# The first batch of an FFT and channel-mix kernel: folds, stages and fillers put in another order

## The chip, the cores and the metric

The kernel runs on one core of a Trainium2 chip. The metric is the device time of one launch in microseconds (us); the median of several runs counts. Instructions of one engine run in the order in which they stand in its queue: PE (TensorE) multiplies, DVE (VectorE) and ACT (ScalarE) compute elementwise and empty PSUM, POOL (GpSimd) computes indices and issues the loads, SP (SyncE) issues the stores.

## The reference

```python
def _attn_ref(x) -> np.ndarray:          # x: 8 x 3072 x 256, float32
    X = np.fft.fft(x, axis=1)
    X = np.fft.fft(X, axis=2)
    return X.real.astype(np.float32)

def _moe_ref(x, mu_k, mu_r, w_k, w_v, w_r) -> np.ndarray:
    B, S, D = x.shape
    x_prev = np.concatenate([np.zeros((B, 1, D), dtype=np.float32), x[:, :-1, :]], axis=1)
    xk = mu_k * x + (1.0 - mu_k) * x_prev
    xr = mu_r * x + (1.0 - mu_r) * x_prev
    k = np.maximum(xk @ w_k, 0.0)
    v = k * k @ w_v
    r = 1.0 / (1.0 + np.exp(-(xr @ w_r)))
    return (r * v).astype(np.float32)
```

The second function takes the first one's result as x. So there is a real part of a two-dimensional Fourier transform of each of the 8 batches, then a mix of each row with the row before it, and three matrix products.

## The kernel before

**Fourier transform, for one batch.** Each batch is loaded in two halves h (0 and 1) as 96 partitions of some rows each: xp by plain loads, xm by gathers of the mirrored rows (lines 119 to 142, all on POOL). `fold` (L144, instructions at L153 and L155, DVE) adds xp and the mirrored xm into p. Stage A of the first batch is `a_sum` (L461, matmuls at L473): products of p with the table w_pm into PSUM, four rows at a time, emptied into the tile a by DVE (L434) or ACT (L436). Stage D (`d_units` L481, matmuls at L488) multiplies a by the table w_eo, two units (`d_half`) or four (`d_item`) at a time, into g_all. Stage C (`c_item` L513, matmuls at L526) multiplies g_all by the table m_cs for some of the 27 slots and empties PSUM into pq (ACT). With `turn_late` a one-row product stands in for a correction that `turned` (L507) makes in g_all later, by means of the table `turn` (L379 to 381). `halves` (L534, instruction at L542), `diff` (L545, L550) and a mix make the inputs x of the matrix products from pq, on DVE. The mix of the first batch's first part is `mix_part` (L579): one SCALAR_TENSOR_TENSOR for each half a (L586). Elsewhere it is `scaled` (L553, TENSOR_SCALAR at L562) and `mixed` (L566, TENSOR_TENSOR at L575).

**Channel mix.** Six chunks of 512 rows for each batch. `k_piece` (L611) takes the products with w_k (L606) in four steps of a chunk and puts them through Relu on ACT (L616); `square` (L620, instruction at L623) squares on DVE; `v_tile` (L637, L644) multiplies by w_v; `r_item` (L625, L630) makes the gate; `v_out` (L648) multiplies both on DVE and stores.

**The tables** w_pm, w_eo and m_cs are computed in the kernel: rows of small integers on DVE (L275 to 297), their outer products on PE (L301) into PSUM, angles u_w, rl and ueo on DVE (L241, which is the line of a helper), sines on ACT (L335 to 341 and L393).

**Fillers.** `keep_busy(n, ps, cols)` (L182, matmuls at L185) issues n matmuls of zeros of 512 or 128 columns; nothing reads their result.

**Order.** `pin_order` (L90) keeps each engine's instructions in the order in which the code issues them. Ahead of the loop (L666 to 734) the first batch's first stages stand written out by hand. In the loop (L813) each step issues a `k_piece`, then what `at(step, ...)` has entered for it, a `v_tile` and the squares; entries of kind "x" (stages A, C, D, `turned`, `r_item`) come ahead of the `v_tile`, others behind it. PSUM has three slots W of 1024 columns and two slots V of 512, handed out in turn.

Of the kernel before, what the change touches and what calls it, by code (L numbers as in the profile page):

```python
# [20 lines left out]
def _v(ap, extra_offset, free_dims):  # L21
    new_ap = [list(ap.ap[0])] + [[s, c] for (s, c) in free_dims]
    return dataclasses.replace(ap, offset=ap.offset + extra_offset, ap=new_ap)
# [16 lines left out]
def kernel(  # L40
# [41 lines left out]
    def ps_v():  # L82
        return ps_slot("V", 2, 512)
# [23 lines left out]
    V = nc.vector  # L107
# [74 lines left out]
    def keep_busy(n, ps, cols=512):  # L182

        for _ in range(n):
            nc.tensor.matmul(out=ps[:, 0:cols], lhsT=zeros,  # L185
                             rhs=_v(zeros, 0, [(0, cols // P), (1, P)]), start=True, stop=True)

    fill = ps_w()
    keep_busy(8, fill)


    mu_row = const.tile([2, 256], FP32)
# [46 lines left out]
    def ts(out, in0, s1, op0, s2=None, op1=None):  # L239
        kw = {} if op1 is None else {"op1": op1}  # L240
        V.tensor_scalar(out=out, in0=in0, scalar1=s1, scalar2=s2, op0=op0, **kw)  # L241
# [78 lines left out]
    def m_outer(ps, j0, j1):  # L320
        n = j1 - j0
        outer(ps[:, 0:64 * n], (Q2, rv(JR, j0, (1, n), (0, 64))),
              (RR, rv(TR, 0, (0, n), (1, 64))), (HQ, rv(ONE, 0, (0, 64 * n))))

    ang_ps = [ps_v(), ps_v()]
    m_outer(ang_ps[0], 0, NJ1)
    outer(prep[:, P_E:P_E + 128], (JR, rv(JR, 0, (1, 2), (2, 64))))
    m_outer(ang_ps[1], NJ1, NJ)
# [26 lines left out]
    ts(ueo, ueo, TURN - 1, ALU.bitwise_and)  # L355
    m_angles(ang_ps[1], NJ1, NJ)

    keep_busy(12, fill)
    ps = ps_v()
    for a in range(2):  # L360
        nc.tensor.matmul(out=ps[:, 2 * a:2 * a + 2], lhsT=mu_p[:, a], rhs=unit, start=True,
                         stop=True)
    V.tensor_copy(out=mu_f.rearrange("p a i -> p (a i)"), in_=ps[:, 0:4])

# [9 lines left out]
               32.0 - 64.0 * c, ADD)  # L376
        ts(rv(TO, 15, (32, 4)), _v(one, 15, [(32, 4)]), 0.0, ADD)

    def turn_table(ps):  # L379
        V.tensor_copy(out=cols, in_=ps[:, 0:2])  # L380
        ts(turn, ramp, cols[:, 0:1], ALU.is_equal, cols[:, 1:2], MUL)

    def rows():
# [48 lines left out]
    def evac(out_ap, in_ap, eng):  # L432
        if eng == "V":
            V.tensor_copy(out=out_ap, in_=in_ap)  # L434
        else:
            nc.scalar.activation(out=out_ap, in_=in_ap, func=AF.Copy)  # L436
# [24 lines left out]
    def a_sum(b, h, i0, eng="A", m=4):  # L461


        if (h, i0) == (0, 0):
            a_tile(b)
        ps = ps_w() if m == 4 else ps_v()
        for i in range(m):
            parts = [(h, i0 + i + 1 - h, 0, 2 * WA, 0, 1)]
            if h and i0 + i == 7:
                parts = [(0, 0, 0, WA, WA, 1), (1, 7, 1, WA, 1, 2)]  # L470
            for half, q, o, n, w, step in parts:
                for k in range(2):
                    nc.tensor.matmul(out=_v(ps, 256 * i + o, [(2 * WA // n, n)]),  # L473
                                     lhsT=p_t[b, half][:, q, 128 * k:128 * k + 128],
                                     rhs=_v(w_pm[0:96], (WA + WB) * k + w,
                                            [(WA + WB, 2), (step, n // 2)]),
                                     start=(k == 0), stop=(k == 1))
        evac(_v(a_t[b], 8 * h + i0, [(16, 2 * WA), (1, m)]),
             _v(ps, 0, [(1, 2 * WA), (256, m)]), eng)

    def d_units(b, ps, u0, n, bank):  # L481

# [94 lines left out]
                        op=ALU.subtract if m else ALU.add)  # L577

    def mix_part(b, j, lo, hi):  # L579


        if lo == 0:
            x_t[b, j, 0] = mix_pool.tile([P, 2, 1536], FP16, name=f"x{j}0")
        n = 64 * (hi - lo)
        for a in range(2):
            V.scalar_tensor_tensor(out=x_t[b, j, 0][:, a, 64 * lo:64 * hi],  # L586
                                   in0=_v(x_t[b], 64 * (26 * a + lo), [(1, n)]),
                                   scalar=mu_f[:, a, j:j + 1],
                                   in1=_v(y_t[b], 64 * (NSL * a + lo), [(1, n)]),
                                   op0=ALU.mult, op1=ALU.add)  # L590
# [77 lines left out]
    eo_sine()  # L668
    eo_rest()
    m_sine(NJ1, NJ2)  # L670
    m_sine(NJ2, NJ)
    keep_busy(4, fill)
    fold(0, 0, 1, 4)
    a_sum(0, 0, 0, "V")
    fold(0, 0, 5, 4)
    a_sum(0, 0, 4)
    loads()
    fill = ps_v()
    keep_busy(10, fill, 128)
    fold(0, 1, 0, 4)  # L680
    a_sum(0, 1, 0)
    keep_busy(4, fill, 128)
    fold(0, 0, 0, 1)
    fold(0, 1, 4, 4)
    a_sum(0, 1, 4, "V", 2)
    a_sum(0, 1, 6, "A", 2)
    turn_rows()
    ps = ps_w()
    keep_busy(6, ps, 128)
    d_half(0, 0, ps_v(), "A")  # L690
    d_half(0, 2, ps_v(), "V")
    for n in range(2):
        outer(ps[:, n:n + 1], (TO + n, rv(ONE, 0, (1, 1))))
    keep_busy(6, ps[:, 512:1024], 128)
    turn_table(ps)
    c_item(0, 0, 5, "A", True)
    c_item(0, 5, 4, "A", True)
    d_item(0, 1)

# [25 lines left out]
    diff(0, 0, 4)  # L727
    mix_part(0, 0, 0, 4)
    halves(0, 5, 9)
    keep_busy(10, ps_w(), 128)  # L730
    k_products(chunks[0], 0, 0, 256)
    k_products(chunks[0], 1, 0, 256)
    diff(0, 4, 8)
    mix_part(0, 0, 4, 8)
    c_item(0, 9, 4, "A", True, True)
    c_item(0, 13, 4, "A", True, True)
    for n, c in enumerate(chunks):
        at(4 * n + (4, 5, 6)[(n < 3) + (n == 0)], r_item, c)

# [2 lines left out]
    at(0, diff, 0, 8, 16)  # L742
    at(0, mix_part, 0, 0, 8, 16)
    at(4, loads_2)
    at(4, d_item, 0, 2)
    at(4, d_item, 0, 3)
    at(4, mix_part, 0, 1, 0, 8)
    at(5, turned, 8, 13)
    at(5, c_item, 0, 17, 8)
    at(5, mirrored_mu)  # L750
    at(5, mix_part, 0, 1, 8, 16)
# [107 lines left out]
```

## Time and profile before

| | us |
|---|---|
| median of 3 runs | 445.52 (445.05 to 446.3) |
| the profiled execution, its own time | 449.81 |
| its span, first to last instruction | 448.0 |
| busy in the span: PE / PEld / DVE / ACT / POOL | 436.6 / 311.8 / 361.0 / 327.5 / 51.6 |

The profile is of one execution. The mean granted clock of PE is 0.988 of full speed over the span. A row of a timeline gives the start, the time from the first instruction's start to the last one's end, engine, line, operation, what it writes and reads, shape and count, and in brackets the engine's idle time before it and what ended it. A row of a group gives busy time, mean duration in ns and idle time before. "x8" counts instructions.

### The profile page before, as it was taken

To read this page: it belongs to the slowest core of one execution; us is meant where nothing else is said; L and a number is where in the kernel's file an instruction comes from. 1 tells how busy PE (TensorE), PEld (TensorE's weight loads), DVE (VectorE), ACT (ScalarE), POOL (GpSimd) and SP (SyncE) were. 2 spreads that over 40 slices of the span, in tenths; PEclk is the share of its full clock that TensorE was granted. 3 is DMA by queue.
4 is the path that set the end of the run, shared out by engine and by line. 5 is a ranking of instruction groups with operands and counts; after the bars stand their busy time and mean duration, and the time that the engine had idled before them with its cause. 6 is when DMAs were issued, how large, how long until landed. Compare 5 with 4: busy or idle time off the path is not lost.

```text
span 448.0 us, 8503 instructions
## 1 busy us (share of the span) xinstructions
PE 436.6 (97%) x3479; PEld 311.8 (70%) x3479; DVE 361.0 (81%) x521; ACT 327.5 (73%) x377; POOL 51.6 (12%) x66
## 2 busy tenths in 40 slices
PE   9798999999999999999999999999999999999995
PEld 3665677677777767777777777777777777676664
DVE  6559999989699887989789887989789755997453
ACT  7558988677777777777777877777777777666661
POOL 7842312001200040001200010000000000000000
PEclk9779999999999999999999999999999999999999
DMA  7994758236823295234932363323223233233334
GB/s 129 173 208 78 149 93 180 51 70 109 171 60 68 50 160 128 53 72 84 184 70 50 71 126 63 67 53 72 62 58 71 48 72 64 55 72 71 72 68 97
DMA packets 34507, 40.93 MB, mean 91 GB/s; under 512 B 3906, under 2 KB 30788, under 8 KB 34468
## 3 DMA queue, kind: packets, MB, share of 16 engines
q1 hardware_dynamic: 27524, 25.05, 24.9%
q0 software_dynamic: 6784, 15.21, 21.2%
q8 instruction: 27, 0.44, 0.4%
q10 hardware_dynamic: 160, 0.13, 0.1%
q14 instruction: 12, 0.10, 0.1%
HBM read 30.41 MB, written 25.17 MB: 124 GB/s over the span
## 4 chain that ended last, share of the span: by engine, by line
PE 91%; DVE 7%; ACT 1%; issue 1%
PE psV L644 35%; PE psW L606 34%; PE psW L630 9%; PE psW L526 3%; PE psW L488 2%; PE psW L185 2%; PE psW L456 2%; DVE k L623 1%; DVE x L586 1%; DVE p L153 1%; DVE d L550 1%; PE psW L473 1%; PE psV L301 1%; DVE o L654 0%; DVE y L542 0%
## 5 line engine op out<-in xcount | busy, mean ns | idle before, releaser
L616 ACT ACTIVATE rl<-psW 128x1024 f16<-128x1024 f32 x192 | 196.1, 1024 | 98.3 <-PE psW L606 93.8
L606 PE MATMUL psW<-x,wk 128*128 128x512 f16 (+1 forms) x776 | 197.7, 377 | 2.2 <-ACT rl L616 0.7
L644 PE MATMUL psV<-wv_sb,k 128*128 128x256 f16 x1536 | 199.3, 273 | 0.3 <-DVE k L623 0.2
L644 PEld LDWEIGHTS <-k 128*128 128x128 f16 x1536 | 146.0, 98 | 28.6 <-DVE k L623 1.1
L623 DVE TENSOR_TENSOR k<-rl 128x2048 f16<-128x2048 f16 (+1 forms) x98 | 117.4, 1200 | 50.5 <-ACT rl L616 46.5
L606 PEld LDWEIGHTS <-wk 128*128 128x128 f16 x776 | 75.7, 98 | 53.2 <-issue 3.2
L654 DVE SCALAR_TENSOR_TENSOR o<-psV,r 128x512 f32<-128x512 f32 (+1 forms) x97 | 66.1, 682 | 16.2 <-PE psV L644 13.7
L575 DVE TENSOR_TENSOR x<-y,t 128x1536 f16<-128x1536 f16 x60 | 57.5, 959 | 2.1
L630 PE MATMUL psW<-wr,x 128*128 128x256 f16 x384 | 49.8, 273 | 0.0
L635 ACT ACTIVATE r<-psW 128x1024 f16<-128x1024 f32 x48 | 48.9, 1018 | 0.8 <-PE psW L630 0.8
L630 PEld LDWEIGHTS <-x 128*128 128x128 f16 x384 | 37.6, 98 | 14.6 <-issue 0.3
L125 POOL DMA_INDIRECT xm<-in_x_dram,idx x25 | 31.5, 1260 | 8.1 <-issue 7.2
L122 POOL DMA_DIRECT2D xp<-in_x_dram x16 | 9.1, 567 | 199.0 <-DVE p L155 184.3
L436 ACT ACTIVATE g_all<-psW 128x1024 f16<-128x1024 f32 (+3 forms) x39 | 28.1, 724 | 1.2 <-PE psW L488 1.2
L436 ACT ACTIVATE pq<-psW 128x768 f16<-128x768 f32 (+5 forms) x32 | 27.5, 860 | 2.0 <-issue 1.3
L436 ACT ACTIVATE a<-psW 128x832 f16<-128x832 f32 x30 | 25.8, 860 | 3.1 <-PE psW L473 3.1
L542 DVE TENSOR_TENSOR y<-pq 128x960 f16<-128x960 f16 (+5 forms) x38 | 18.7, 533 | 3.9 <-ACT pq L436 3.7
L526 PEld LDWEIGHTS <-g_all 128*128 128x128 f16 (+1 forms) x216 | 15.3, 99 | 8.9 <-ACT g_all L436 1.1
L153 DVE TENSOR_TENSOR p<-xp,xm 96x2304 f16<-96x2304 f16 (+3 forms) x19 | 20.9, 1102 | 0.0
L562 DVE TENSOR_SCALAR t<-d,mu_m 128x1536 f16<-128x1536 f16 x32 | 19.8, 619 | 0.0
L488 PEld LDWEIGHTS <-a 128*128 128x128 f16 x208 | 14.7, 101 | 7.4 <-issue 0.7
L526 PE MATMUL psW<-m_cs,g_all 128*128 128x128 f16 (+2 forms) x204 | 18.1, 227 | 0.9 <-ACT g_all L436 0.9
(98 smaller groups left out, 195.7 us busy)
## 6 DMA issues: line engine op xcount, KB each, us to landing
out_dram<-o SPq DMA_DIRECT2D x190, 128.0 KB, 2.4
xp<-in_x_dram POOLq DMA_DIRECT2D x8, 432.0 KB
xp<-in_x_dram POOLq DMA_DIRECT2D x8, 384.0 KB
wv_sb<-in_moe_w_v_dram POOLq DMA_DIRECT2D x1, 512.0 KB
xm<-in_x_dram,idx POOLq DMA_INDIRECT x25
out_dram<-o ACTq DMA_DIRECT2D x2, 64.0 KB
out_dram<-o SPq DMA_DIRECT2D x2, 64.0 KB
wk<-in_moe_w_k_dram,row_i POOLq DMA_INDIRECT x4
```

The lines of the kernel that those rows point to most:

```text
L125: nc.gpsimd.indirect_dma_start(dst, None, src, bass.IndirectOffsetOnAxis(ap=idx, axis=0))
L153: V.tensor_tensor(out=p[:, q0:q0 + n], in0=xp[:, q0:q0 + n], in1=_v(xm, o + 256, [(-256, n), (-1, 256)]), op=ALU.add)
L436: nc.scalar.activation(out=out_ap, in_=in_ap, func=AF.Copy)
L526: nc.tensor.matmul(out=ps[0:m, o:o + 64 * k], lhsT=g_all[:, u, 128 * min(f, 1):128 * min(f, 1) + m], rhs=m_cs[:, f % 2, sl:sl + k], start= ...
L575: V.tensor_tensor(out=dst, in0=_v(y_t[b], 64 * (NSL * a + lo + 3 * m), [(1, n)]), in1=_v(x_t["t", a], 64 * lo, [(1, n)]), op=ALU.subtract ...
L606: nc.tensor.matmul(out=st["k", ds][:, 512 * hs + lo:512 * hs + hi], lhsT=wk_sb[m][a][:, 128 * fc:128 * fc + 128], rhs=xk[:, a, 512 * i + l ...
L616: nc.scalar.activation(out=st["rl"][:, 2 * ds:2 * ds + 2], in_=st["k", ds].rearrange("p (f t) -> p f t", f=2), func=AF.Relu, bias=0.0, sca ...
L623: V.tensor_tensor(out=k2_t[c][:, lo:hi], in0=r, in1=r, op=ALU.mult)
L630: nc.tensor.matmul(out=ps[:, 256 * tb:256 * tb + 256], lhsT=x_t[b, 1, m][:, a, 512 * i + 128 * tb: 512 * i + 128 * tb + 128], rhs=wr_sb[m] ...
L635: nc.scalar.activation(out=st["r", c], in_=ps, func=AF.Sigmoid)
L644: nc.tensor.matmul(out=st["v", tb - h][:, 256 * h:256 * h + 256], lhsT=k2_t[c][:, fc, 128 * tb:128 * tb + 128], rhs=wv_sb[:, fc], start=(f ...
L654: V.scalar_tensor_tensor(out=o.rearrange("p a b -> p (a b)")[:, 0:256 * n], in0=st["v", t0][:, 0:256 * n], scalar=16.0, in1=st["r", c][:, ...
```

## The change

The early part of the first batch is put in another order, and the counts of fillers differ:

- Fillers: ahead of the outer products 4 instead of 8 (512 columns), and one more between them; ahead of the product for mu 5 instead of 12, and 7 behind it; 16 + 6 + 6 of 128 columns along stage A instead of 4 (of 512 columns) and 10 + 4 + 6 + 6; 20 instead of 10 ahead of the first `k_products`.
- Stage A of half 0: matmuls and evacuation of the first four rows are apart (`a_evac`). On DVE the second fold stands ahead of the evacuation, on PE the second `a_sum` comes directly behind the first, and on ACT the last pair of sines (`m_sine(NJ2, NJ)`) behind that second one's evacuation.
- Stage D of units 0 to 7 at once in four `d_half`, the last two in one PSUM tile; before, units 4 to 7 came as a `d_item` behind the first stage C pieces.
- Stage C of slots 0 to 16 directly behind it; before, slots 9 to 16 came behind the first `k_products`.
- The table `turn`: its two products in step 1 and its DVE operation in step 2 of the loop. The other `d_item` one step earlier (3), `turned` too (4).
- `mix_part` outside the first eight rows of the first part (five calls) by `scaled` and `mixed`.

```diff
-    keep_busy(8, fill)
+    keep_busy(4, fill)
...
     ang_ps = [ps_v(), ps_v()]
+    keep_busy(1, fill)
...
-    keep_busy(12, fill)
+    keep_busy(5, fill)
...
+    keep_busy(7, fill)
...
-    def turn_table(ps):
+    def turn_cols():
+        ps = ps_w()
+        for n in range(2):
+            outer(ps[:, n:n + 1], (TO + n, rv(ONE, 0, (1, 1))))
         V.tensor_copy(out=cols, in_=ps[:, 0:2])
+
+    def turn_table():
         ts(turn, ramp, cols[:, 0:1], ALU.is_equal, cols[:, 1:2], MUL)
...
+        a_ps[b, h, i0] = ps
+        if eng:
+            a_evac(b, h, i0, eng, m)
+
+    a_ps = {}
+
+    def a_evac(b, h, i0, eng, m=4):
         evac(_v(a_t[b], 8 * h + i0, [(16, 2 * WA), (1, m)]),
-             _v(ps, 0, [(1, 2 * WA), (256, m)]), eng)
+             _v(a_ps[b, h, i0], 0, [(1, 2 * WA), (256, m)]), eng)
...
     def mix_part(b, j, lo, hi):
+        if j or lo > 4:
+            for a in range(2):
+                scaled(b, j, 0, a, lo, hi)
+                mixed(b, j, 0, a, lo, hi)
+            return
...
     m_sine(NJ1, NJ2)
+    fold(0, 0, 1, 4)
+    a_sum(0, 0, 0, "")
+    fold(0, 0, 5, 4)
+    a_evac(0, 0, 0, "V")
+    a_sum(0, 0, 4)
     m_sine(NJ2, NJ)
-    keep_busy(4, fill)
-    fold(0, 0, 1, 4)
-    a_sum(0, 0, 0, "V")
-    fold(0, 0, 5, 4)
-    a_sum(0, 0, 4)
     loads()
     fill = ps_v()
-    keep_busy(10, fill, 128)
+    keep_busy(16, fill, 128)
     fold(0, 1, 0, 4)
     a_sum(0, 1, 0)
-    keep_busy(4, fill, 128)
+    keep_busy(6, fill, 128)
...
     turn_rows()
-    ps = ps_w()
-    keep_busy(6, ps, 128)
+    keep_busy(6, ps_w(), 128)
     d_half(0, 0, ps_v(), "A")
     d_half(0, 2, ps_v(), "V")
-    for n in range(2):
-        outer(ps[:, n:n + 1], (TO + n, rv(ONE, 0, (1, 1))))
-    keep_busy(6, ps[:, 512:1024], 128)
-    turn_table(ps)
+    ps = ps_w()
+    for u, eng in ((4, "A"), (6, "V")):
+        d_half(0, u, ps[:, 256 * u - 1024:256 * u - 512], eng)
     c_item(0, 0, 5, "A", True)
     c_item(0, 5, 4, "A", True)
-    d_item(0, 1)
+    c_item(0, 9, 4, "A", True, True)
+    c_item(0, 13, 4, "A", True, True)
...
-    keep_busy(10, ps_w(), 128)
+    keep_busy(20, ps_w(), 128)
...
-    c_item(0, 9, 4, "A", True, True)
-    c_item(0, 13, 4, "A", True, True)
...
-    at(4, d_item, 0, 2)
-    at(4, d_item, 0, 3)
+    at(1, turn_cols)
+    at(2, turn_table)
+    at(3, d_item, 0, 2)
+    at(3, d_item, 0, 3)
     at(4, mix_part, 0, 1, 0, 8)
-    at(5, turned, 8, 13)
+    at(4, turned, 8, 13)
```

## The prediction

> **What bounds the kernel now.** I read the page first (the slices, then the chain that ended last by engine), then the chain in order of time, then clock and transfers in short windows, then the timelines of DVE, PE and ACT up to 55 us.
>
> ```profile
> PEclk9779999999999999999999999999999999999999
> PE 91%; DVE 7%; ACT 1%; issue 1%
> ```
> ```profile
> 49.56 1.14 DVE k L623
> ...
> 52.64 0.87 PE psV L644 x8
> ```
>
> 91% of the chain is PE; in order of time the chain leaves DVE at about 50.7 and from 52.64 on is almost all PE. Matmuls behind that point are untouched by the change, so what is won before it moves the end. The start is another matter: the clock is low in slices 1 and 2, and there the chain changes engine at nearly every step. The windows (columns: busy of PE, PEld, DVE, ACT, POOL, then clock, DMA share, GB/s) say where:
>
> ```profile
> 17.00:18.00 1.00, 1.00 (x10) 0.92 (x8) 0.77 (x2) 0.62 (x1) 0.76 (x1) 0.52 1.36 177
> 27.00:28.00 1.00, 0.96 (x12) 0.77 (x11) 1.00 (x4) 0.43 (x1) 0.70 (x2) 0.86 1.00 197
> ```
> ```profile
> 1.00 3.59 PE L185 MATMUL psW<-zeros 128*128 128x512 f16 x8 [1.00 <-DVE xm L208]
> 5.62 0.31 PE L301 MATMUL psW<-rw 1*128 1x128 f16 x1
> 7.14 4.27 PE L185 MATMUL psW<-zeros 128*128 128x512 f16 x12
> 11.87 1.04 PE L185 MATMUL psW<-zeros 128*128 128x512 f16 x4
> 15.83 0.89 PE L473 MATMUL psW<-w_pm,p 96*128 96x208 f16 x8 [1.93 <-DVE p L155]
> 17.17 1.59 PE L473 MATMUL psW<-w_pm,p 96*128 96x208 f16 x8
> 18.98 2.24 PE L473 MATMUL psV<-w_pm,p 96*128 96x208 f16 x10
> 22.12 1.04 PE L488 MATMUL psV<-w_eo,a 128*128 128x128 f16 x8 [0.25 <-issue]
> 29.08 1.12 PE L526 MATMUL psV<-m_cs,g_all 128*128 128x128 f16 x12
> ```
>
> A share of 0.52 in the window from 17 and 0.86 in that from 27 put the half clock at 17.04 to 27.28, 10.24 us. It follows the idle stretch of 1.93 us ahead of 15.83. The price is plain: the same eight matmuls take 0.89 us at 15.83 and 1.59 at 17.17. Fillers show a slow start too: 0.45 us each at 1.00 (3.59 / 8), 0.26 at 11.87, though the clock column has 1.00 there; full speed begins inside the twelve at 7.14. The Trainium skill, page "TensorE: Matmul & The Clock Gate", Part 1, says that the clock is judged over a free-running window of about 3.41 us, low by default, full after a busy window; 10.24 us are three such windows, so by that rule the trace agrees.
>
> DVE is the other line; brackets give idle time and what ended it:
>
> ```profile
> 3.14 0.37 DVE L241 TENSOR_SCALAR rw<-rw 1x64 f16<-1x64 f16 x1
> 5.96 0.37 DVE L241 TENSOR_SCALAR u_w<-psW 128x26 int32<-128x26 f32 x3 [2.46 <-PE psW L301]
> 10.93 0.69 DVE L241 TENSOR_SCALAR rl<-rl 128x1024 int32<-128x1024 int32 x1
> 12.06 0.69 DVE L153 TENSOR_TENSOR p<-xp,xm 96x1024 f16<-96x1024 f16 x1
> 13.94 1.02 DVE L434 CAST a<-psW 128x832 f16<-128x832 f32 x1 [0.98 <-PE psW L473]
> 15.69 0.68 DVE L153 TENSOR_TENSOR p<-xp,xm 96x1024 f16<-96x1024 f16 x1
> 17.63 0.17 DVE L155 TENSOR_TENSOR p<-xp,xm 96x4 f16<-96x4 f16 x1
> 25.71 0.63 DVE L542 TENSOR_TENSOR y<-pq 128x320 f16<-128x320 f16 x2 [1.08 <-ACT pq L436]
> 31.77 0.76 DVE L542 TENSOR_TENSOR y<-pq 128x512 f16<-128x512 f16 x2 [2.28 <-ACT pq L436]
> 34.63 2.48 DVE L623 TENSOR_TENSOR k<-rl 128x1024 f16<-128x1024 f16 x4
> 37.04 1.40 DVE L586 SCALAR_TENSOR_TENSOR x<-d,mu_f,y 128x512 f16<-128x512 f16 x2
> ```
>
> From 25.71 to 50.7 DVE idles once for long, 2.28 us ahead of 31.77, until the pq of the late stage C pieces. So there DVE sets the pace, and whatever moves 25.71 forward moves the rest.
>
> **The change part by part.**
>
> *Fillers ahead of the tables.* Eight become four, one is added behind the small products: three fewer ahead of the product at 5.62, on which u_w waits 2.46 us. At 0.43 to 0.45 us each that is 1.3: u_w starts at 4.66. Its inputs allow it: the last row of rw is done at 3.51, the product now starts at 4.3. DVE's work behind u_w has no other wait, so the last mask ends at 10.3, not 11.62; the mu products stand behind five fillers, not twelve, and are done by about 8.7, so the copy to mu_f no longer waits. First fold: 12.06 becomes 10.4.
>
> *Is the data there?* In the order of the queue the first two folds need 432 and 384 KB.
>
> ```profile
> xp<-in_x_dram POOLq DMA_DIRECT2D x8, 432.0 KB
> xp<-in_x_dram POOLq DMA_DIRECT2D x8, 384.0 KB
> ```
> ```profile
> 5.00:10.00 5.00, 5.00 (x14) 1.70 (x13) 3.90 (x14) 3.64 (x9) 3.65 (x12) 1.00 0.97 175
> 10.00:15.00 5.00, 3.79 (x22) 1.92 (x20) 3.59 (x8) 4.70 (x9) 4.39 (x5) 1.00 1.09 172
> ```
>
> At 175 GB/s 875 KB come between 5 and 10 alone, so these 816 are there at 10.4 even if nothing came before 5. The other half needs 768 more and a gather of single rows (some 48): at 172 GB/s all of it by 14.4 on the same bound, and earlier by what did come before 5; those folds are due at 13.2 to 14.5. POOL's and SP's order is unchanged. So I cost the loads at nothing; if they came after all, each microsecond late is a microsecond lost.
>
> *Folds ahead of the evacuation.* Now the second fold waits behind the CAST (13.94, itself waiting 0.98 for PE), and PE idles 1.93. After: folds at 10.4 and 11.2, PE's first product 11.35 to 12.25 and its second directly behind, the CAST at 12.3 to 13.3. The three folds left take 2.11 us (15.69 to 17.80), so the last ends at 15.3 instead of 17.80: 2.5 earlier. On ACT two sines move behind the second evacuation; they delay only the third, which is done before the last one.
>
> *The clock.* From 11.3 on PE has products and fillers with only sub-microsecond gaps, so I take full clock from about 10 to 12 us on. From the last fold to stage D took 4.32 us (17.80 to 22.12): PE came late from its slow products, and ten matmuls took 2.24. After: 1.12 for the ten, and ACT's 0.54:
>
> ```profile
> 21.52 0.54 ACT L436 ACTIVATE a<-psV 128x416 f16<-128x416 f32 x1 [1.86 <-PE psV L473]
> 24.98 1.44 ACT L436 ACTIVATE pq<-psW 128x640 f16<-128x640 f32 x2 [1.34 <-issue]
> 30.65 1.08 ACT L436 ACTIVATE pq<-psV 128x512 f16<-128x512 f32 x2 [2.06 <-PE psV L526]
> ```
>
> with hand-offs 1.9 us, so stage D starts at 17.2, 4.9 earlier.
>
> *Stage D of eight units, stage C of 17 slots.* Stage D to the first y took 3.59 us (22.12 to 25.71). After, the instruction order holds a new wait: the last half's matmuls write the PSUM tile that ACT is reading for the third half, and all of stage C stands behind them on PE. So: 0.4 for the first half, 1.1 for ACT's two evacuations of 512 columns (two in 1.08 at 30.65), 0.3 for the last half, 0.6 for six matmuls of C, 0.72 for pq, 0.1 of hand-offs: 3.2. First y at 20.4, 5.3 earlier. The four pq are done by 22; DVE asks for the last two at 24.1, so the 2.28 goes. Next late would be ACT's Relu for the squares, four times 1.0 from about 24.5, ready as DVE takes them up.
>
> *DVE up to the squares.* Its own work from first y to squares is 34.63 - 25.71 - 2.28 = 6.6; then 2.4 for the squares and 0.35 for the two table operations that move between them (DVE was idle where they stood). They end at 20.4 + 6.6 + 2.4 + 0.35 = 29.8 instead of 37.04: 7.2 earlier. Can PE keep up?
>
> ```profile
> 25.00:30.00 5.00, 4.58 (x44) 3.41 (x42) 3.64 (x10) 2.30 (x3) 3.97 (x5) 0.77 1.07 208
> 30.00:35.00 5.00, 3.70 (x21) 1.72 (x22) 3.16 (x6) 4.35 (x6) 0.00 (x0) 1.00 1.14 209
> 35.00:40.00 5.00, 3.84 (x35) 2.21 (x33) 4.96 (x10) 3.73 (x6) 0.00 (x0) 1.00 0.09 17
> ```
>
> From 25 to 40 it was busy 12.1 us, 1.1 of it the price of the half clock up to 27.28; ten fillers more are 0.9 (0.093 each by the twelve at 29.08): 11.9. DVE needs 14.3 - 2.28 + 0.5 = 12.5 for the same stretch. DVE stays the bound, narrowly.
>
> *Mixes in two operations.* Five parts, ten pairs:
>
> ```profile
> L586 DVE SCALAR_TENSOR_TENSOR x<-d,mu_f,y 128x512 f16<-128x512 f16 x10 | 7.0, 742 | 0.1
> ```
> ```profile
> L562 DVE TENSOR_SCALAR t<-d,mu_f 128x1536 f16<-128x1536 f16 x28 | 17.1, 611 | 0.0
> L550 DVE TENSOR_TENSOR d<-y 128x512 f16<-128x512 f16 x2 | 0.8, 424 | 0.1
> L539 DVE TENSOR_SCALAR pq<-pq 1x64 f16<-1x64 f16 x7 | 1.1, 162 | 0.0
> ```
>
> One operation costs 0.66 to 0.70 in the row (two in 1.40, overlapping). The pair is a TENSOR_SCALAR of 512, between 0.16 (64) and 0.61 (1536), by the line between them 0.30, then 0.04 of waiting for it and 0.34 for the addition: 0.68. Ends: 0.54 to 0.99, so -1.4 to +3.3 us over ten; I take +0.03 each, 0.3 in all. The Trainium skill, "VectorE: DVE Perf Modes", section on the TRN2 errata, speaks against splitting: a fixed cost per instruction, about 150 cycles of 0.96 GHz as measured there; by it the scaling would be some 0.29 us (an estimate from that page) and the sum the same.
>
> *Sum.* 7.2 - 0.3 = 6.9. I give back 0.9 for hand-offs that the records do not explain: at 30.65 ACT starts both pq, though PE's twelve matmuls end at 30.20 and the first six about 0.5 before. So 6.0: span 448.0 to 442.0, the profiled execution 449.81 to 443.8. The timed runs (445.05 to 446.3) lie 4.3 below that execution; I take the difference as the same in both kernels: 445.52 - 6.0 = **439.5 us**.
>
> **The rivals.**
>
> *The clock rises a step later.* Fewer fillers up front, and the mu products (0.6 us, two rows) cut the later row. If full clock comes at 17 instead of 10 to 12, four products lose 0.7 each, of which the CAST and the folds pass on 0.7, the product of the second half 0.7, and its late hand-offs 0.7 to 1.0: 2.2 less, 441.7. For it: the twelve fillers at 7.14 were unbroken. The skill's clock page asks for about 4 us without a break, and the unbroken stretches here are shorter; by that rule this rival holds. Against: the break is small, and the window ending at 27.28 released the clock with a mix of small matmuls. Chance 0.13.
>
> *The timed runs of before had less half clock than the profiled one.* Then only the order is won: 2 to 3 us (folds 1.6, the 2.28, less what the clock hid): 443. For it: timed runs lie 4.3 lower. Against: they agree within 1.25. Chance 0.08.
>
> *The pairs cost their upper end,* 3.3: 442.5, and more of the same if DVE work that was hidden behind 52 us comes to the front. 0.05.
>
> *Slower: full clock does not come before about 34 us.* PE's 3.6 us of products up to first y become 7.2, with late hand-offs as above, so y comes at 25.0, 0.7 earlier than before; with the 2.28 and less 0.6 for table operations and pairs DVE's line is 2.4 ahead. But PE's margin of 0.6 is soon gone, and then each microsecond at half clock costs half of one. The lead and the margin, 3.0, are used up at a release 6 us behind y, at 31; with one at 34 to 36 the time is 447 to 448. For it: behind 17 us the clock stayed low for two windows in which PE looked nearly full. Against: 48 fillers, where there were 36, stand behind the second product. 0.04.
>
> *The change does not do what it says:* excluded by the instruction order, in which both folds stand ahead of the CAST.
>
> **How the numbers follow.** Forecast (438 to 441.2) 0.68; the rivals 0.13, 0.08, 0.05, 0.04; 0.02 is left for more than 7.5 us. The range takes in the first three rivals in part: 437.6 to 443.3. Under 0.3% (1.3 us) a measurement of this kernel can't tell from no change: faster 0.91, same 0.05 (parts of the second and third), slower 0.04.
>
> **What would show it.** In the profile after: u_w near 4.7; first fold near 10.4; no idle of over 1 us on PE between 12 and 17; clock 1.00 from 13 on at the latest; stage D near 17.2; first y near 20.4, no idle over 1 us on DVE up to the squares; their end near 30; the pairs at 0.68. Wrong if 0.5 shows behind 17, if DVE waits for pq or data, or if the lead at 30 us is lost by 84.

## The result and the profile after

The changed kernel takes **444.23 us** (median of 6, 443.51 to 444.68) against 445.51 (445.05 to 446.3) for the kernel before in the same set: ratio 0.9969, 95% interval 0.9956 to 0.9982. The gain is 1.3 us, where 6.0 had been forecast.

The profiled executions tell another story: span 448.0 before and 441.7 after, 6.3 less, and the forecast had 6.0 less. The timed medians do not follow, and the experiments below show that the agreement of the spans is largely luck: the profile of the kernel before has late hand-offs (results of PE that reach their reader well behind the product's end), that of the changed kernel has none, and this is not the change's doing. The page of the changed kernel, granted clock by slices and shares of the chain:

```profile
PEclk9999999999999999999999999999999999999999
PE 86%; DVE 5%; DMA 4%; POOL 2%; issue 1%; ACT 1%; POOLq 0%
```

The two slices at 7 are gone, and the chain now leads through DMA and POOL for 6% of the span, which it did not before: in the start-up it now hangs on loads. The timelines of DVE and of PE, after (start, length, ..., idle before and what ended it):

```profile
4.88 0.37 DVE L241 TENSOR_SCALAR u_w<-psW 128x26 int32<-128x26 f32 x3 [1.38 <-PE psW L301]
10.42 0.68 DVE L153 TENSOR_TENSOR p<-xp,xm 96x1024 f16<-96x1024 f16 x1
13.10 1.02 DVE L441 CAST a<-psW 128x832 f16<-128x832 f32 x1 [1.00 <-PE psW L480]
15.95 0.17 DVE L155 TENSOR_TENSOR p<-xp,xm 96x4 f16<-96x4 f16 x1
16.75 0.59 DVE L441 CAST a<-psV 128x416 f16<-128x416 f32 x1 [0.62 <-PE psV L480]
21.11 0.56 DVE L556 TENSOR_TENSOR y<-pq 128x320 f16<-128x320 f16 x2 [0.48 <-ACT pq L443]
24.74 0.75 DVE L556 TENSOR_TENSOR y<-pq 128x512 f16<-128x512 f16 x2
26.26 0.35 DVE L576 TENSOR_SCALAR t<-d,mu_f 128x512 f16<-128x512 f16 x1
26.64 0.42 DVE L589 TENSOR_TENSOR x<-y,t 128x512 f16<-128x512 f16 x1
26.99 0.35 DVE L576 TENSOR_SCALAR t<-d,mu_f 128x512 f16<-128x512 f16 x1
29.24 1.29 DVE L642 TENSOR_TENSOR k<-rl 128x1024 f16<-128x1024 f16 x2
```
```profile
12.18 1.59 PE L480 MATMUL psW<-w_pm,p 96*128 96x208 f16 x16
16.18 1.07 PE L480 MATMUL psV<-w_pm,p 96*128 96x208 f16 x10
17.88 0.34 PE L502 MATMUL psV<-w_eo,a 128*128 128x128 f16 x3 [0.30 <-ACT a L443]
```

Read down the first column: the first fold at 10.42 (forecast 10.4), the last fold done at 16.12 (15.3), stage D at 17.88 (17.2), first y at 21.11 (20.4), the third y at 24.74 without a wait, squares done at 30.53 (29.8). From the CAST on all of it is 0.7 to 0.8 us later than forecast.

Behind the first stored tile both kernels are alike. The rows of the output's first issue, before and after:

```profile
47.79 2.40 SPq L662 DMA_DIRECT2D out_dram<-o  x3
```
```profile
41.56 1.36 SPq L681 DMA_DIRECT2D out_dram<-o  x2
```

From there to the end it is 448.0 - 47.79 = 400.2 and 441.7 - 41.56 = 400.1 us, and 400.1 to 400.2 in every other trace but that of c_ahead_held (400.9). **The time is the start-up plus a constant**, so an execution of 445.5 has its first issue near 43.6. And in every execution whose span is listed the time lies 1.7 to 1.9 us above it, so spans and times tell the same. The kernel before was profiled in an execution 4.3 us above its median, the changed one in its fastest of six.

### The profile page after: what moved, and what is told of

Its sections match the earlier page's. It is cut to its first block, busy times and chain, and to the rows that moved or that the text cites. A ratio compares the mean times of both kernels' runs of the same rounds, so it can differ in the third digit from the quotient of the medians.

```text
span 441.7 us, 8525 instructions
## 1 busy us (share of the span) xinstructions
PE 431.9 (98%) x3484; PEld 309.4 (70%) x3484; DVE 361.0 (82%) x532; ACT 326.7 (74%) x377; POOL 50.9 (12%) x66
## 4 chain that ended last, share of the span: by engine, by line
PE 86%; DVE 5%; DMA 4%; POOL 2%; issue 1%; ACT 1%; POOLq 0%
PE psV L663 36%; PE psW L625 35%; PE psW L649 9%; DMA xp<-in_x_dram 2%; PE psW L502 2%; PE psW L540 2%; PE psW L463 2%; DMA wr<-in_moe_w_r_dram,row_i 2%; DVE k L642 1%; POOL xm L125 1%; DVE x L589 1%; POOL wk L125 1%; DVE d L564 1%; DVE p L153 1%; DVE t L576 1%
## 5 line engine op out<-in xcount | busy, mean ns | idle before, releaser
L589 DVE TENSOR_TENSOR x<-y,t 128x1536 f16<-128x1536 f16 (+1 forms) x70 | 61.8, 882 | 2.4
L443 ACT ACTIVATE g_all<-psW 128x1024 f16<-128x1024 f32 (+4 forms) x39 | 27.7, 712 | 0.0
L576 DVE TENSOR_SCALAR t<-d,mu_f 128x1536 f16<-128x1536 f16 (+1 forms) x38 | 20.6, 542 | 0.1
```

The costliest lines, as they stand in the source:

```text
L576: V.tensor_scalar(out=dst, in0=src, scalar1=mu, scalar2=None, op0=ALU.mult)
L589: V.tensor_tensor(out=dst, in0=_v(y_t[b], 64 * (NSL * a + lo + 3 * m), [(1, n)]), in1=_v(x_t["t", a], 64 * lo, [(1, n)]), op=ALU.subtract ...
```

## The experiments

The question: what did that execution of the kernel before have that the others lack, and what is each part of the change worth without it? The five sets ran on four chips, on which the kernel before took 449.4 to 450.4 us: as much as the profiled 449.81, and not the 445.5 of the result. The record names no chip for the result and the first two profiles. Times are compared within a set, and where they are not, the text says so. The recorded ratios can differ from the quotient of the medians by up to 0.0024 (after_again: 448.75 / 450.28 is 0.9966), so differences of 1 us between sets mean little.

| kernel | us, median (range) | ratio to the kernel before (95%) |
|---|---|---|
| before_again | 449.72 (446.93 to 451.31) | 0.9968 (0.9935 to 1.0002) |
| after_again | 448.75 (448.29 to 450.99) | 0.9988 (0.9959 to 1.0017) |
| before_cover | 450.59 (448.74 to 456.35) | 1.0011 (0.9981 to 1.0041) |
| after_one_op | 448.61 (447.36 to 449.68) | 0.9969 (0.9941 to 0.9998) |
| after_look | 448.53 (448.14 to 449.39) | 0.9983 (0.9958 to 1.0008) |
| held_loads | 444.93 (444.3 to 445.53) | 0.9889 (0.9846 to 0.9932) |
| wide_fill | 446.49 (445.84 to 448.08) | 0.9943 (0.9915 to 0.9971) |
| stage_a | 448.86 (446.74 to 452.78) | 0.999 (0.9955 to 1.0025) |
| before_held | 446.4 (445.7 to 447.21) | 0.9931 (0.9911 to 0.9951) |
| stage_a_held | 443.91 (443.58 to 444.73) | 0.9878 (0.9856 to 0.9899) |
| one_op_held | 444.84 (444.3 to 446.77) | 0.9903 (0.9879 to 0.9926) |
| wide_held | 445.09 (444.25 to 445.83) | 0.9904 (0.9885 to 0.9923) |
| dc_held | 447.47 (446.42 to 448.29) | 0.9932 (0.9908 to 0.9956) |
| c_ahead_held | 445.19 (443.14 to 445.56) | 0.986 (0.9825 to 0.9894) |
| stage_a_held_2 | 444.1 (443.53 to 445.38) | 0.9856 (0.9821 to 0.9891) |
| held_loads_2 | 445.23 (444.75 to 445.57) | 0.9877 (0.9843 to 0.991) |
| eight_early | 443.88 (443.47 to 444.17) | 0.9885 (0.9849 to 0.992) |
| four_early | 443.21 (443.01 to 443.57) | 0.9868 (0.9833 to 0.9904) |

### Both kernels once more, more cover, one operation

before_again and after_again are the two kernels unchanged. The other two edits:

```diff
 (before_cover)
     fold(0, 0, 1, 4)
     a_sum(0, 0, 0, "V")
+    keep_busy(8, fill)
     fold(0, 0, 5, 4)
```
```diff
 (after_one_op)
-        if j or lo > 4:
-            for a in range(2):
-                scaled(b, j, 0, a, lo, hi)
-                mixed(b, j, 0, a, lo, hi)
-            return
```

> The kernel before, unchanged, run again. Theory A (the profiled execution of before was an unlucky one, with 10.24 us at half clock in the middle, and most executions have less): the runs' spans stand at 443.2 to 444.7 us, each about 1.8 below its time, with a mean clock above 0.99, and a new profile shows a shorter half-clock stretch or one in another place. Theory B (the profiler adds some 4 us to before and not to the kernel after, or the lead is lost in executions without a profile): the new profile shows 448 us again with a clock near 0.988, while the times stay at 445.5.

> The changed kernel, unchanged, run again. Theory A: spans of 441.5 to 443, clock 0.997 to 1.0; time of the median 444.2; the first r product of the loop near 36 us. Theory B: the same.

> The kernel before with eight fillers of 512 columns in PE's idle stretch of 1.93 us ahead of the second stage A product; nothing else. Theory A (half clock costs the start its time whenever that idle falls badly): no half clock behind 13 us in any execution, the first r product near 39 to 40 us instead of 42.46, times 1 to 2 us below the ordinary runs of before and with less scatter, about 444. Theory C (ordinary executions of before have full clock there anyhow): the time is that of before, 445.5, within 0.5.

> The changed kernel with mix_part in one operation everywhere, as before. By the pair's price of the prediction (+0.03 us each, eight of them ahead of 52 us): 0.2 to 0.3 us faster than the kernel after, so 443.9. Rival: the pairs cost up to 0.33 each in effect, or gain by freeing something else: then 2 us faster or slower.

The second trace of the kernel before has half clock from 14.5 to 17.9 only, not 10.2 us of it; its first fold stands at 10.94, not 12.06. With a third of the half clock its time is nearly the same (449.34 against 449.81), so the half clock alone doesn't make those 4.3 us. Neither theory's numbers came: here both kernels take longer, and by about as much, 449.7 against 445.5 and 448.75 against 444.2. And the changed kernel's second trace has something that its first has not: PE stops for 2.18 us inside the last products of stage A, and stage D starts at 21.65. Eight fillers more did nothing (half clock came all the same, from 22.2 to 29.0 us), and of the one-operation form nothing is told apart (0.14 us between the medians). The next set was made to find that stop.

### What stops TensorE: the loads or its own instructions

after_look is the changed kernel; stage_a is the kernel before with the front half of the change alone (fillers of the front, folds first, 16 and 6 fillers). The two others:

```diff
 (held_loads, on the changed kernel)
-        load_xh(1, 0)
         for a in range(2):
             gather(wr_sb[0][a], moe_w_r, row_i[:, a:a + 1])
-        load_xh(1, 1)
...
+    def late_loads():
+        x_tiles(1, 0)
+        V.memset(xp_t[1, 0][0:1, 0, 0:1], 0.0)
+        load_p(1, 0)
+        load_m0(1)
+        load_m(1, 0, 0, 8, idx_8[:, 1, 0:1])
+        load_xh(1, 1)
...
     mix_part(0, 0, 4, 8)
+    late_loads()
```
```diff
 (wide_fill, on the changed kernel)
-    keep_busy(16, fill, 128)
+    keep_busy(4, fill)
...
-    keep_busy(20, ps_w(), 128)
+    keep_busy(5, ps_w())
```

> The changed kernel unchanged, for its trace and the clocks of its executions beside those of the kernel before on one chip. Every trace so far has its end 400.15 to 400.23 us behind the first output's issue, so the time is the start-up alone. Theory U (the profiled execution of the kernel before was out of the ordinary: its half clock and its late hand-offs cost 4 us more than in its other executions, and the change gains the order only): 0.996 to 0.9985 of the kernel before, the first y at 21 to 22 us where TensorE's results are handed over promptly. Theory N (the forecast of 6.0 us holds wherever the kernel before is undisturbed too): 0.987. If hand-offs are late here as in the second look at this kernel (2.18 us idle in the last products of stage A), the first y comes at 25 to 26.5 us and the clock has a half stretch of 6.8 us.

> The changed kernel with the loads of x for the second batch held back behind the second mix of the first one (wk, wv and wr still load at once). Theory L (TensorE's results reach the other engines late, by 0.7 to 2.9 us between 16 and 30 us, because these loads run then): the idle 2.18 us in the last products of stage A is gone, the first y at 21 to 22 us, and 2 to 4 us less than the changed kernel on the same chip if that one shows late hand-offs there; the same within 0.5 us if it shows none. Rival F (TensorE's own stream of instructions is what arrives late, as it runs out of the 8 KB that it last fetched): the idle time stays, the same within 0.7 us. Fold of the second batch has 15 us between the loads' new start and its use, so no wait there.

> The changed kernel with its small fillers of 128 columns (16, 6, 6 and 20) as a quarter as many of 512 columns (with a 256 for the odd half): the same columns, 35 fewer products and as many fewer weight loads ahead of the first chunk. Rival F (the stream of instructions): the idle time ahead of the last products of stage A goes or moves behind stage D, and 1 to 3 us less than the changed kernel where that shows it. Theory L (the loads): the idle time stays at the same place and the time is the same within 0.7 us. Fillers in the wide form end no sooner, so a gain has no other source.

> The kernel before with the front half of the change alone: the fillers of the front placed anew, both folds ahead of the evacuation, 16 and 6 fillers; stages D and C, the half of c_item behind the second mix and the one-operation mixes stay as they were. Theory U (order only, small): the last fold ends 1.7 to 2.5 us sooner than in the kernel before, stage D begins as much sooner, but the second half of stage C is still behind the second mix, so the squares gain less than stage D: 0.995 to 1.000 of the kernel before. Theory N (the forecast's step: 2.5 us at the last fold, and the clock a step sooner, carried whole): 0.990 to 0.994.

On one chip, held_loads takes 3.6 us less than the changed kernel, wide_fill 2.0 less. The timelines of the changed kernel (after_look), PE and then DVE:

```profile
17.03 0.52 PE L480 MATMUL psV<-w_pm,p 96*128 96x208 f16 x4
18.88 0.70 PE L480 MATMUL psV<-w_pm,p 96*128 96x208 f16 x6 [1.32 <-PE psV L480]
20.96 0.62 PE L502 MATMUL psV<-w_eo,a 128*128 128x128 f16 x8 [1.06 <-DVE rw L374]
```
```profile
19.59 0.59 DVE L441 CAST a<-psV 128x416 f16<-128x416 f32 x1 [2.74 <-PE psV L480]
25.40 0.56 DVE L556 TENSOR_TENSOR y<-pq 128x320 f16<-128x320 f16 x2 [0.48 <-issue]
```

The four products end at 17.55; DVE, idle since 16.85, may take them only at 19.59. **The result is handed over 2.0 us late**, where the profile of the changed kernel at the top has 0.04 (products done at 16.71, CAST at 16.75). The lateness is in PE's signal: the trace's semaphore records have it at 19.57. PE itself waits in the same way, by the program's waits for its own filler that used that PSUM slot: that is the 1.32. What ACT and DVE hand over is prompt in the same trace: stage D starts 0.06 us behind ACT's evacuation, 20.36 to 20.90. The same place in held_loads:

```profile
16.91 1.06 PE L486 MATMUL psV<-w_pm,p 96*128 96x208 f16 x10
```
```profile
17.48 0.65 DVE L447 CAST a<-psV 128x416 f16<-128x416 f32 x1 [0.62 <-PE psV L486]
21.86 0.56 DVE L562 TENSOR_TENSOR y<-pq 128x320 f16<-128x320 f16 x2 [0.48 <-ACT pq L449]
```

No late hand-off is left, the first y comes 3.5 us sooner. What differs is in the windows from 16 to 24 us, after_look and held_loads (last three columns: clock, DMA share, GB/s):

```profile
16.00:24.00 8.00, 3.69 (x50) 3.24 (x48) 2.78 (x11) 4.24 (x7) 5.57 (x7) 1.00 1.18 195
```
```profile
16.00:24.00 8.00, 6.96 (x92) 5.57 (x91) 5.59 (x19) 5.84 (x10) 0.00 (x0) 1.00 0.65 83
```

The changed kernel loads 195 GB/s, with POOL issuing for 5.57 us, and PE works 3.69 us of the 8; held_loads loads 83 GB/s, POOL issues nothing, PE works 6.96. Most of this difference in load lies behind 20 us, though. Around the stop itself the rows are these, of after_look, of held_loads and of the first trace of the changed kernel:

```profile
16.50:18.50 2.00, 1.06 (x15) 0.90 (x13) 0.32 (x2) 1.65 (x3) 1.62 (x2) 1.00 1.31 176
```
```profile
16.50:18.50 2.00, 1.81 (x24) 1.50 (x21) 1.23 (x7) 1.99 (x4) 0.00 (x0) 1.00 1.23 164
```
```profile
16.50:18.50 2.00, 1.70 (x26) 1.53 (x24) 1.27 (x7) 1.33 (x3) 1.69 (x3) 1.00 1.35 182
```

held_loads loads 164 GB/s here, nearly as much. And the first trace, with 182 GB/s, with POOL issuing and with the same products, has no late hand-off up to 40 us, where the eight other traces without held loads all have some, the first profile of the kernel before among them (its first pq at 30.65, in the prediction's rows, starts 1.0 us behind the end of its products). So the runs show what removes the late hand-offs, and not what makes them. Holding the second batch's loads removes them. Wide fillers do it in part: with wide_fill the stop in stage A is gone (its ten products run through in 1.07 us), but the evacuations of stage D are late, by 1.1 to 2.2 us. In eight_early below 158 GB/s run from 24 to 32 us beside products that mostly have 256 and 512 columns, without one late hand-off. Which path is shared (the traffic, POOL's issuing, the stream of PE's instructions), and what the first trace of the changed kernel was spared, no run tells. The Trainium skill, page "Runtime: NRT & Kernel Launch", section "Instruction fetch mechanics", says that crossing a block of instructions costs little and is mostly hidden; held_loads, with the same stream of PE's instructions and no stop, agrees, and for the time beside the loads no run here shows it.

stage_a came out as theory U had it (0.999, and the interval from 0.9955 leaves theory N's 0.990 to 0.994 out). But PE idles 1.41 us in the same products there, so this is not the part's own price. The parts were taken again with the loads held.

### The parts of the change, undisturbed

before_held and stage_a_held are the kernel before and stage_a, one_op_held is after_one_op, wide_held is wide_fill, each with the loads held as in held_loads.

> The kernel before with its loads of x for the second batch held back behind the second mix, as in held_loads. There the late hand-offs are gone, so the two kernels can be compared undisturbed. Theory U (order alone, 1 to 2 us): 445.7 to 447.2 us, stage D at 19 to 20 us, first y at 22 to 23.5, half clock short or absent. Theory N (the forecast's 6 us are in the kernel before as such, by its half clock): 450 to 451 us, half clock of 6 us or more behind 14 us, stage D at 21 to 22, first y at 25 to 26.

> Stage A's half of the change (fillers of the front, folds first) with the loads held back. Between before_held and held_loads (444.93 us): its distance from before_held is what stage A's half is worth undisturbed, its distance to one_op_held what stages D and C are worth. Theory U: 0.3 to 0.8 us below before_held (the last fold 0.5 us sooner by the trace), the rest with stages D and C. If stages D and C are all of it, the same as before_held within 0.3.

> The changed kernel with every mix part in one operation, the loads held back. Forecast's price of the pairs: 0.02 us each, 0.3 in all at most, against held_loads. By the trace of the changed kernel (0.73 us from pair to pair against 0.66) 0.07 each, 0.28 on the four pairs ahead of the first chunk's squares: 444.65 where held_loads has 444.93. The other way: the same within 0.1, if another engine holds the squares.

> The changed kernel with both mends: loads held back and wide fillers. With prompt hand-offs the fillers' form has nothing left to give: 444.5 to 445.1 us, as held_loads. If many small products cost something of their own, beyond the late hand-offs, 443 to 444.

Holding the loads takes 3.2 us off the kernel before, as theory U had it (but stage D starts at 20.86, not at 19 to 20). Stage A's half of the change takes another 2.5 (446.40 to 443.91), which none of the theories had; stages D and C in the changed order give 0.9 back (444.84). wide_held, with 445.09 against 444.93 of held_loads (other chip), shows that the fillers' form is worth nothing once hand-offs are prompt. What the pairs cost in time stays between 0.1 and 0.25: one_op_held lies 0.1 below held_loads (other chip) and 0.25 below wide_held (same chip, fillers differ), and its own runs spread over 2.5 us.

Stage A first. The timelines of DVE, before_held and stage_a_held:

```profile
13.19 0.69 DVE L153 TENSOR_TENSOR p<-xp,xm 96x1024 f16<-96x1024 f16 x1
23.40 0.56 DVE L548 TENSOR_TENSOR y<-pq 128x320 f16<-128x320 f16 x2 [0.74 <-ACT pq L442]
27.94 0.82 DVE L548 TENSOR_TENSOR y<-pq 128x512 f16<-128x512 f16 x2 [0.82 <-ACT pq L442]
30.87 2.52 DVE L629 TENSOR_TENSOR k<-rl 128x1024 f16<-128x1024 f16 x4
```
```profile
10.39 0.68 DVE L153 TENSOR_TENSOR p<-xp,xm 96x1024 f16<-96x1024 f16 x1
13.84 1.02 DVE L442 CAST a<-psW 128x832 f16<-128x832 f32 x1 [1.76 <-PE psW L481]
21.44 0.56 DVE L557 TENSOR_TENSOR y<-pq 128x320 f16<-128x320 f16 x2 [0.74 <-ACT pq L444]
25.98 0.82 DVE L557 TENSOR_TENSOR y<-pq 128x512 f16<-128x512 f16 x2 [0.82 <-ACT pq L444]
28.91 2.52 DVE L638 TENSOR_TENSOR k<-rl 128x1024 f16<-128x1024 f16 x4
```

The kernel before has its first fold anywhere from 10.9 to 13.2 us. By the clock records of its traces it goes with the clock's first rise: 4.3 us in before_again (fold at 10.94), 10.2 in the first profile (12.06), 12.6 in before_held (13.19, behind a copy to mu_f that waits 1.46 us for PE). With the front's fillers thinned the rise comes at 12.0 to 15.2 us in all traces, and the fold at 10.39 to 10.51 all the same. The Trainium skill, page "TensorE: Matmul & The Clock Gate", Part 1, has the clock judged over free-running windows; a rise whose place differs from execution to execution of one program agrees with that. What the folds' new order saves is then mostly paid to the late rise: the first sixteen products take up to 3.0 us and the CAST stands at 13.84. Where the kernel before has an early rise (dc_held has its front, with the rise at 4.4 us), its last fold ends at 16.63, no later than stage_a_held's at 16.85; but then half clock from 14.7 to 18.1 goes with PE's idle 1.94 us ahead of the second products, and stage D starts at 20.22 (in before_held the same idle, 1.92 us, has full clock behind it, so the idle alone doesn't decide it). So the kernel before pays about 2 us either way: stage D at 20.86 (before_held) against 18.90 (stage_a_held), and on one chip 20.22 (dc_held) against 18.26 (held_loads_2).

### What the order of stages D and C is worth

dc_held is before_held with the change's order of stages D and C and nothing else. c_ahead_held is stage_a_held with this edit, and the last two let the loads go sooner:

```diff
 (c_ahead_held)
     d_item(0, 1)
+    keep_busy(10, ps_w(), 128)
+    c_item(0, 9, 4, "A", True, True)
+    c_item(0, 13, 4, "A", True, True)
...
-    keep_busy(10, ps_w(), 128)
     k_products(chunks[0], 0, 0, 256)
...
     late_loads()
-    c_item(0, 9, 4, "A", True, True)
-    c_item(0, 13, 4, "A", True, True)
```
```diff
 (eight_early on one_op_held, four_early on c_ahead_held)
     mix_part(0, 0, 0, 4)
+    late_loads()
...
     mix_part(0, 0, 4, 8)
-    late_loads()
```

> The kernel before with the change's order of stages D and C alone (eight units of stage D at once, 17 slots of stage C behind them, 20 fillers, the outer products of the turn later), loads held back as in before_held; stage A and the mixes as before. Theory V (undisturbed, this order costs: stage D to the first y 3.2 us with it, 2.5 without, and the wait of the third y for pq, which it saves, is 0.8 us, not 2.28): 0.4 to 1.0 us above before_held's 446.4, so 446.8 to 447.4. Theory O (the order gains by itself, as the forecast had it: 1.0 us at the first y and the wait): 1 us or more below, 444.5 to 445.4. On this kernel the first fold still hangs on the first rise of the clock.

> stage_a_held with stage C's slots 9 to 16 moved from behind the second mix to ahead of the first chunk's products, behind the second group of stage D, which stays a group of its own. Theory V: the first y stays at 2.5 us behind stage D, the third y has no wait for pq (0.8 us there in stage_a_held), and the first products of the chunk wait for the 1.1 us of stage C: 443.2 to 443.9, 0 to 0.6 below stage_a_held. Rival: TensorE is what ends last there (no idle time from 23 to 31 us but 0.8), so the order of its work moves nothing: the same within 0.2; or the chunk's first products come 0.8 us later and the squares with them: 0.5 above.

> stage_a_held once more, on the chip of the other three. Theory V: 0.4 to 1.2 us below the changed kernel with the same holding (443.9 against 444.9 in two different sets). If that difference was the chip's: the same within 0.3.

> held_loads once more, as the reference for stage_a_held_2 and c_ahead_held: 444.5 to 445.2.

> one_op_held (the changed order of stages D and C, one operation in every mix) with the loads let go one mix sooner, behind the first mix instead of the second. In one_op_held the fold of the second batch waits 0.90 us for xm, and TensorE idles 1.20 us behind it, in stage_a_held only 0.33 and 0.39, so a part of what the order seems to cost may be the holding's. Theory V (the order costs by the first y, 0.6 us later): 444.0 to 444.7 against stage_a_held's 443.9 to 444.1. Theory W (the whole cost of about 1 us was the wait for the held loads): 443.4 to 444.0. If the late hand-offs come back with loads that run from 24 us: 445.2 or more, and the first rl evacuations late.

> c_ahead_held (stage D in two groups, stage C whole ahead of the products) with the loads let go behind the first mix. There the fold waits 1.24 us for xm, TensorE idles 1.30 us at 34 us and half clock follows in the profiled execution (445.35), while two of six executions took 443.1. Theory V: with the wait gone all of them lie at 442.6 to 443.3, about 1 us below eight_early, which differs in the groups of stage D (and the place of the fillers and of the turn) alone. Theory W (the groups of stage D cost nothing): the same as eight_early within 0.3. If the late hand-offs come back: 444 or more.

The cost repeats: dc_held is 1.1 above before_held's 446.4 (other chip), and held_loads_2 1.1 above stage_a_held_2 on one chip. But it is not the order's own. The timeline of one_op_held, and behind it that of eight_early:

```profile
22.06 0.56 DVE L562 TENSOR_TENSOR y<-pq 128x320 f16<-128x320 f16 x2 [0.48 <-ACT pq L449]
30.07 1.29 DVE L643 TENSOR_TENSOR k<-rl 128x1024 f16<-128x1024 f16 x2
33.59 1.36 DVE L153 TENSOR_TENSOR p<-xp,xm 96x2304 f16<-96x2304 f16 x1 [0.90 <-DMA xm<-in_x_dram,idx]
```
```profile
18.21 0.62 PE L508 MATMUL psV<-w_eo,a 128*128 128x128 f16 x8 [0.30 <-ACT a L449]
19.78 0.38 PE L508 MATMUL psW<-w_eo,a 128*128 128x128 f16 x4 [0.73 <-ACT g_all L449]
32.04 1.35 DVE L153 TENSOR_TENSOR p<-xp,xm 96x2304 f16<-96x2304 f16 x1
```

Against stage_a_held the first y is 0.62 later (22.06, 21.44), and the squares end at 31.36 against 31.43: **what the order loses at the first y it wins back at the third, and no more**. The loss is the wait of 0.73 in the row at 19.78 and all that stands behind it: stage D to first y takes 3.23 us in this order in each of its seven traces with prompt hand-offs, and 2.54 or 2.55 in the five of the other. The gain is the third y's wait, 0.82 there (not 2.28), less the table operations that now stand among the squares. The difference of 0.9 to 1.1 came from the held loads, as far as times of different chips can show it: the second batch's fold waits 0.90 us for xm here, 0.33 in stage_a_held (and 0.48 in held_loads, where no wait was expected). Let go one mix sooner (eight_early), the wait is gone and the time is 443.88, that of stage_a_held (443.91 and 444.10, other chips). So theory V's price of the order was wrong, and theory W right in the main, for what stage_a_held's own 0.33 leaves open.

c_ahead_held shows the same wait at its worst (1.24 us, half clock from 34 us in the profiled execution; most executions at 445, two at 443.1, where 443.2 to 443.9 was expected). four_early has it still:

```profile
20.59 0.56 DVE L557 TENSOR_TENSOR y<-pq 128x320 f16<-128x320 f16 x2 [0.74 <-ACT pq L444]
27.14 2.52 DVE L638 TENSOR_TENSOR k<-rl 128x1024 f16<-128x1024 f16 x4
32.14 1.36 DVE L153 TENSOR_TENSOR p<-xp,xm 96x2304 f16<-96x2304 f16 x1 [1.16 <-DMA xm<-in_x_dram,idx]
```

Its squares end at 29.66, 1.1 ahead of eight_early's, and the fold starts at 32.14 against 32.04: the second batch's data take the lead back in the two profiled executions (443.57 and 443.47). By the medians it is the fastest kernel of all, **443.21**, 0.7 below eight_early on the same chip and 1.3% below the kernel before there: stage D in groups of four, stage C whole ahead of the chunk's products, the changed front, loads let go behind the first mix.

## Why the prediction was wrong

- **The step that failed is the last of the sum**: "I take the difference as the same in both kernels". The sum of 6.0 starts from a profile with half clock and late hand-offs (449.81) and ends at a start-up without them (443.8), so the 4.3 us between that profile and the timed runs are in the 6.0 already, and the last line takes them off a second time. The runs show that these 4.3 us are not the change's to win: from the result to the chip of the first set the kernel before goes from 445.5 to 449.7 and the changed kernel from 444.2 to 448.75. Kernel against kernel, 1.3 us were measured in the result, and 0.9 to 1.5 by the medians on two other chips.
- Why both kernels have them: there the changed kernel has late hand-offs and half clock too, and its first y comes at 25.40 and 26.05, no earlier than the 25.14 of before_again. Holding the loads removes the late hand-offs and takes 3.2 us off the one kernel and 3.6 off the other, to 446.4 and 444.9, near the 445.5 and 444.2 of the result. That the timed runs of the kernel before were spared them likewise is the likely reading, and not shown: none of them was traced.
- The spans, 6.3 apart where 6.0 had been forecast, agree by luck: one has the late hand-offs, the other hasn't.
- A rival had the right direction (443, with a chance of 0.08, "they agree within 1.25"): that the timed runs agree with each other was evidence for it, not against. It too gave the order 2 to 3 us, where 1.3 were measured.
- Fillers ahead of the tables: right. u_w at 4.88 (4.66 forecast), first fold 10.42 (10.4). What it is worth depends on the execution: 0.5 to 2.8 us by the folds of the kernel before.
- The clock "from about 10 to 12 us on": late. It rises at 12.15 in the profile and at 12 to 15 in others; the CAST comes at 13.0 to 13.8, not 12.3. The rival with the later rise (2.2 us, 0.13) was half true: 0.8 us here.
- Last fold 2.5 and stage D 4.9 earlier: 1.7 and 4.2 in the two profiles; undisturbed stage D gains 1.96 (both pairs above). The 4.32 us from last fold to stage D were half clock and late hand-offs; undisturbed the kernel before takes 1.98 (18.88 to 20.86 in before_held).
- Stage D to first y 3.2: measured 3.23. But the 3.59 it replaced are 2.54 undisturbed, so a gain of 0.4 is a loss of 0.7.
- The wait of 2.28: gone as forecast; undisturbed it is 0.82. Both numbers were right in the trace and wrong as a price.
- The pairs: 26.26 to 26.99, so 0.73 us each against 0.66, +0.07 where +0.03 was taken; in time 0.1 to 0.25 was seen, within the scatter.
- Hand-offs "that the records do not explain": 0.9 was given back once. They are a matter of up to 2.9 us each, in both kernels on the chips of the experiments. The ratios there, 0.9983 and 0.9988, have intervals that take in 1, so what they take of the gain stays open. The prediction costs the loads at nothing, by when their data arrive; through the hand-offs they cost 3.2 and 3.6 us there.
- The lead was kept from 30 us on, as forecast.

Undisturbed, the sum is 2.0 us at stage D for stage A's half (2.2 to 2.5 in time), nothing for the order of D and C, and 0.1 to 0.25 against it for the pairs. That is about 1 us more than the 1.3 measured in the result. What the kernel before does in those executions stays open, and with it this last 1 us.

## What to carry to other kernels

Hold the profiled execution against the median before pricing anything from it: if it is 1% off, profile and median may come from different conditions, and a stall that the profile shows is worth what it costs where the median was taken. Never take off both the stall and the difference. Where everything behind some point is constant (about 400.15 us here), compare that point's start over several traces. And loads that are issued early because they can be are not free: these, let go some 13 us later (POOL's first at 25.90 instead of 12.87), were worth 3.2 and 3.6 us on the chips with late hand-offs, more than twice the whole change.

## What the runs showed of the hardware

On the chips of the experiments PE's results reached DVE, ACT and PE's own next instruction up to 2.9 us late (after_again, in the last products of stage A), between 16 and 31 us, in stretches with 176 to 210 GB/s of loads and many products of 128 or 208 columns, in wide_fill by 0.6 to 0.9 us behind products of 256 columns too. With the second batch's loads held they were within 0.1 up to 33 us, though 164 GB/s were still loaded around 17 us; and in the first trace of the changed kernel they were prompt under 182 GB/s. So load rate and product size alone don't settle it. The clock column doesn't show the lateness (1.00 from 16 to 24 us in after_look): the gap between a product's end and its reader's start does. The first rise of the clock came anywhere from 4.3 to 12.6 us in five traces with the same front of the program, and at 10.2 and 4.3 in two of one and the same program.
